# Output weights in dead columns of the spatial weights, loaded in the kv stage; four output buffers; two banks for the last spatial halves; a reordered start

## The chip, the cores and the metric

The kernel runs on one core of a Trainium2 chip. The metric is the time of one execution on the device, in microseconds, as the median of several executions. The span of a profiled execution (first to last instruction) is about 1.7 us shorter than its time.

## The reference

One input `x` (2048 tokens, 512 wide) goes through two mixers, and a gate blends them. Cut to what matters (the softmax, GELU and layer-norm helpers are the usual ones):

```python
g = sigmoid((x * gate_w).sum(-1, keepdims=True))

# A: linear attention, 32 heads of 16
q, k, v = split(x @ wqkv)                                  # per head
phi_q = concat(softmax(q @ w_phi), softmax(-(q @ w_phi)))  # and phi_k likewise
kv = phi_k.T @ v ;  z = phi_k.sum(over tokens)
a  = ((phi_q @ kv) / (phi_q @ z + 1e-6)) @ wo

# B: gated MLP with a spatial matmul over the 2048 tokens
z1, z2 = halves(gelu(x @ w_in))                            # 688 columns each
u = z1 * (w_sp @ layernorm(z2) + b_sp)
b = u @ w_out

out = g * a + (1 - g) * b
```

## The kernel before

It has three stages. The first computes `z1` and `z2` and folds `w_phi` into the q and k weights. The second, the kv stage, goes over 16 token tiles, accumulates `kv`, and runs one *spatial half* per tile (half of the 688 columns of `w_sp @ z2` for one output tile). The third runs the attention of each tile, the remaining spatial halves, the remaining q tiles, and the output matmuls, which add both mixers in one accumulator. Stores come in groups of four tiles.

The start. The first two tiles are transposed on TensorE; both halves of tile 1 go through one PSUM tile:

```python
tp1 = psA.tile([P, 2, 2 * CH], BF16, name="tp1", tag=next_turn("zp", 3))
# ... warm-up matmuls, transposes of tile 0 ...
one(0, 0, 0)              # one(tile, slab, half): one 128x344 matmul with w_in
for h in range(2):
    x_T(1, 2 * h, 2 * h + 2,
        tp1[:, h, 0:2 * P].rearrange("p (d n) -> p d n", n=P), on_act=h == 1)
one(0, 1, 0)
warm_up(2, P)
one(1, 0, 0)
one(1, 1, 0)
gate_T()                  # puts gate_w beside the weights, as a column of the second halves
for dt in range(2):
    one(0, dt, 1)
    one(1, dt, 1)
one(0, 2, 0)
one(1, 2, 0)
# ...
```

The output weights (1.9 MB) are loaded after the kv stage, into SBUF that the kv stage frees, on ScalarE's queue:

```python
def load_out_weights():
    slabs = outw.tile([P, 11 + NDT, D], BF16, name="slabs")
    # ... w_main, w_rem, wo_t are views of slabs ...
    nc.gpsimd.memset(w_rem, 0.0)
    nc.scalar.dma_start(out=wo_t, in_=A_wo.rearrange("(g p) n -> p g n", p=P))
    # ... four more nc.scalar.dma_start for w_out ...
```

One output tile is nine or ten matmuls of 512 columns. The rows that are left over of `w_out` are added per group, and then ScalarE evicts the four tiles of the group one after the other, each into one of two `ob` buffers, from which a DMA stores it:

```python
def ba_store(acc, tt, c0, c1, on_dve):
    ob = work.tile([P, c1 - c0], BF16, name=f"ob{c1 - c0}")      # pool of 2
    # ... last tile's tail on VectorE ...
        nc.scalar.activation(out=ob[:, :], in_=acc, func=AF.Copy, scale=g_inv[:, tt:tt + 1])
        nc.scalar.dma_start(out=dst, in_=ob[:, :])
```

The third stage, in which one bank serves all q tiles and one all spatial halves:

```python
gg_next(mm_tile())                      # one spatial half, evicted by VectorE
w_main, w_rem, wo_t = load_out_weights()
nq = len(Q_AT)                          # 6 q tiles were done in the kv stage
q_bank, g_bank, *acc_banks = [next_turn("mm", 6) for _ in range(6)]
attn_tile(0)                            # o -> DMA transpose -> oT
for i in range(NT - 1):
    if i + nq < NT:
        q_tile(i + nq, bank_tile(q_bank))   # ScalarE reads the bank twice (exp of +x and -x)
    gg_next(bank_tile(g_bank))
    attn_tile(i + 1)
    if i > 0:
        ba_step(i - 1)                  # output matmuls: needs oT and uT
ba_tile(14)
ba_tile(15, cuts=(0, 384, D))
```

The softmax here doesn't subtract the row's maximum and nothing guards it: scores larger than these inputs give would overflow.

## Time and profile before

| | before |
|---|---|
| time, median | 212.78 us (3 runs, 212.43 to 212.85) |
| span of the profile | 211.2 us |
| TensorE busy | 202.3 us, 96% |
| VectorE, ScalarE, GpSimd busy | 131.4, 75.4, 46.5 us |
| mean granted clock | 1.0 |

The page of the profile of the kernel before: busy microseconds by engine (PE is TensorE), and the span in 40 slices of 5.28 us, in which a digit is the busy share in tenths.

```profile
PE 202.3 (96%) x1438; PEld 121.6 (58%) x1456; DVE 131.4 (62%) x282; ACT 75.4 (36%) x122; POOL 46.5 (22%) x78
...
PE   7999999999999999999999996999989999899994
...
DMA  6999999999912024142221499753544368254342
```

TensorE has something to do almost all the time. The list of what its matmuls waited for is short. The columns are: engine and line that waited, what released it, microseconds in total, number of waits, longest wait. Line 460 is a spatial half, 369 a q or k tile, 497 and 499 the output matmuls.

```profile
PE mm L497 <- DMA oT<-o: 1.7, 1, 1.7
PE mm L369 <- ACT eq L373: 1.0, 1, 1.0
...
PE mm L460 <- DVE ucat L465: 0.6, 1, 0.6
PE tp L286 <- DVE xT L292: 0.4, 1, 0.4
PE zp L196 <- DVE w_z L297: 0.3, 1, 0.3
```

A matmul's wait says who came last, not why it was late. For that one follows the chain of waits (start us, duration us, what), here cut to the three places in the third stage where TensorE was not the one that everything waited for:

```profile
125.79 5.78 DMA oT<-o
131.61 1.04 PE mm L497 x4
...
150.28 0.69 ACT ob L513
150.98 2.43 DMA out_dram<-ob
153.50 0.70 ACT ob L513
...
155.81 1.09 ACT eq L373 x2
156.95 0.38 PE mm L369
...
174.36 4.09 DMA out_dram<-ob
...
180.88 1.09 ACT eq L373 x2
181.99 1.23 DVE zs L377
...
183.83 0.56 DVE ucat L465
184.44 2.49 PE mm L460 x16
```

The first place is the DMA transpose of `o` at 125.79, which took 5.78 us. In the second, an eviction (line 513) waits for a store that takes 2.43 us to release an `ob` buffer (ScalarE stands idle for 1.40 us of it); after this eviction and one more ScalarE comes to the exponentials of a q tile, and only then is the q bank free for line 369. In the third, the store takes 4.09 us and ScalarE waits 3.05, and there VectorE's reduction of the q tile (line 377) comes late too, stands before the eviction of a spatial half (line 465) in VectorE's program, and so line 460 gets its only bank late.

What the gaps cost is read from TensorE's own timeline as the distance between two starts, less what the same distance is elsewhere without a gap: 1.91 us at 131.61, 1.16 us at 156.95, 0.75 us at 184.44. This is a little more than the list of waits says, because a matmul's end in the profile reaches into the next one.

### The profile page before, as it was taken

Reading aid. Unit: us, or ns where it says so; the run is one execution under the profiler, and the core shown is the slowest. Engines: PE = TensorE matmul, PEld = TensorE weight load, DVE = VectorE, ACT = ScalarE, POOL = GpSimd, SP = SyncE. Lnnn points to the kernel's source line nnn. Section 1 sums busy time; section 2 is a strip of 40 time slices with the busy share of each in tenths; the row PEclk is TensorE's granted clock in tenths of the full one; section 3 lists DMA queues with packets and bytes.
Section 4 is the critical chain, followed back from the end, with each engine's and each line's share of the span. In section 5 each row is a group of like instructions: output and inputs, shape, how many; then the busy total and the mean of one; then the engine's idle time right before and its main releaser. Section 6 shows DMA issues by size and latency. Waiting matters only on the chain.

```text
span 211.2 us, 3762 instructions
## 1 busy us (share of the span) xinstructions
PE 202.3 (96%) x1438; PEld 121.6 (58%) x1456; DVE 131.4 (62%) x282; ACT 75.4 (36%) x122; POOL 46.5 (22%) x78
## 2 busy tenths in 40 slices
PE   7999999999999999999999996999989999899994
PEld 3666667765665555656555664555445555565642
DVE  3477685856977586979797669455356563443330
ACT  3666666676222333232323222222251122301322
POOL 7020202020623324424252422122204220100000
PEclk9999999999999999999999999999999999999999
DMA  6999999999912024142221499753544368254342
GB/s 189 267 137 198 250 290 215 274 274 211 260 37 42 0 39 79 21 77 51 41 50 37 75 288 220 137 112 74 121 116 90 75 113 128 75 112 90 101 112 75
DMA packets 88970, 27.20 MB, mean 129 GB/s; under 512 B 82968, under 2 KB 88952, under 8 KB 88952
## 3 DMA queue, kind: packets, MB, share of 16 engines
q1 hardware_dynamic: 84208, 22.43, 54.8%
q10 hardware_dynamic: 4712, 4.53, 7.3%
q8 instruction: 11, 0.18, 0.4%
q14 instruction: 7, 0.06, 0.1%
q0 software_dynamic: 32, 0.00, 0.0%
HBM read 4.41 MB, written 2.10 MB: 31 GB/s over the span
## 4 chain that ended last, share of the span: by engine, by line
PE 86%; DMA 6%; ACT 3%; DVE 1%; issue 1%; ACTq 1%; DVEq 0%
PE mm L460 31%; PE zp L196 18%; PE mm L369 12%; PE mm L499 7%; PE mm L409 7%; PE mm L497 5%; DMA out_dram<-ob 3%; DMA oT<-o 3%; ACT ob L513 2%; PE kvacc L425 2%; PE zp L227 2%; PE at L473 1%; ACT eq L373 1%; PE mm L502 1%; PE pq L321 1%
## 5 line engine op out<-in xcount | busy, mean ns | idle before, releaser
L460 PE MATMUL mm<-z2all,wspT 128*128 128x344 bf16 x512 | 79.9, 309 | 0.6 <-DVE ucat L465 0.6
L460 PEld LDWEIGHTS <-wspT 128*128 128x128 bf16 x512 | 49.0, 98 | 26.5 <-issue 1.3
L196 PE MATMUL zp<-w_z,xT 128*128 128x344 bf16 (+1 forms) x256 | 39.8, 309 | 0.3 <-DVE w_z L297 0.3
L373 ACT ACTIVATE eq<-mm 128x512 bf16<-128x512 f32 x32 | 17.4, 594 | 53.2 <-PE mm L369 25.2
L377 DVE TENSOR_REDUCE zs<-eq 128x64 f32<-128x1024 bf16 x16 | 19.5, 1219 | 24.0 <-ACT eq L373 24.0
L196 PEld LDWEIGHTS <-xT 128*128 128x128 bf16 x256 | 24.5, 98 | 11.5 <-issue 0.4
L465 DVE SCALAR_TENSOR_TENSOR ucat<-mm,bT,z1all 128x344 bf16<-128x344 f32 x32 | 17.5, 547 | 21.7 <-PE mm L460 21.7
L386 POOL TENSOR_TENSOR eq<-eq,ratio 128x512 bf16<-128x512 bf16 x16 | 16.9, 1058 | 52.8 <-DVE ratio L385 41.7
L373 ACT ACTIVATE ek<-mm 128x512 bf16<-128x512 f32 x32 | 17.3, 600 | 27.2 <-PE mm L369 27.2
L513 ACT ACTIVATE ob<-mm,g_inv 128x512 bf16<-128x512 f32 (+1 forms) x16 | 10.9, 680 | 34.6 <-PE mm L502 24.0
L377 DVE TENSOR_REDUCE zs<-ek 128x64 f32<-128x1024 bf16 x16 | 19.3, 1208 | 2.8 <-ACT ek L373 2.8
L369 PEld LDWEIGHTS <-xT 128*128 128x128 bf16 x128 | 12.2, 98 | 14.0 <-issue 1.3
L499 PE MATMUL mm<-slabs,uT 128*128 128x512 bf16 (+2 forms) x85 | 20.1, 366 | 0.0
L497 PE MATMUL mm<-slabs,oT 128*128 128x512 bf16 (+2 forms) x62 | 15.8, 365 | 2.1 <-DMA oT<-o 1.7
L369 PE MATMUL mm<-wq_p,xT 128*128 128x512 bf16 x55 | 16.0, 379 | 1.5 <-ACT eq L373 1.0
L386 POOL TENSOR_TENSOR ek<-ek,ratio 128x512 bf16<-128x512 bf16 x16 | 16.9, 1058 | 2.0 <-DVE ratio L385 1.2
L409 PE MATMUL mm<-wv_sb,xT 128*128 128x512 bf16 x64 | 16.4, 379 | 0.0
L369 PE MATMUL mm<-wk_p,xT 128*128 128x512 bf16 x61 | 16.1, 379 | 0.2
L214 DVE BATCH_NORM_STATS2 bn<-z2all 128x6 f32<-128x344 bf16 x32 | 14.9, 502 | 0.0
L211 ACT ACTIVATE z2all<-zp 128x688 bf16<-128x688 f32 x16 | 11.8, 744 | 7.0 <-PE zp L196 6.6
L266 ACT ACTIVATE z1all<-zp 128x688 bf16<-128x688 f32 x16 | 11.9, 744 | 6.7 <-PE zp L196 6.7
L499 PEld LDWEIGHTS <-uT 128*128 128x128 bf16 x85 | 8.1, 98 | 9.2
(80 smaller groups left out, 148.9 us busy)
## 6 DMA issues: line engine op xcount, KB each, us to landing
out_dram<-ob ACTq DMA_DIRECT2D x15, 128.0 KB, 1.9
slabs<-in_B_w_out_dram ACTq DMA_DIRECT2D x2, 640.0 KB, 8.2
w_z<-in_B_w_in_dram SPq DMA_DIRECT2D x2, 344.0 KB, 4.6
w_z<-in_B_w_in_dram ACTq DMA_DIRECT2D x3, 172.0 KB, 3.3
wv_sb<-in_A_wqkv_dram SPq DMA_DIRECT2D x1, 512.0 KB, 4.5
slabs<-in_A_wo_dram ACTq DMA_DIRECT2D x1, 512.0 KB, 3.8
xs<-in_A_x_dram SPq DMA_DIRECT2D x2, 128.0 KB, 3.3
xs<-in_A_x_dram SPq DMA_DIRECT2D x1, 256.0 KB, 5.0
```

The source lines that it names most:

```text
L196: nc.tensor.matmul(zp[:, j, 0:n], lhsT=xT[:, dt, tt * P:(tt + 1) * P], rhs=wt[:, dt, j * HF:j * HF + n], start=(dt == 0), stop=(dt == NDT ...
L214: nc.vector.bn_stats(out=bn6[:, tt, j, :], in_=z2v[:, j, :])
L369: nc.tensor.matmul(ps[:, :], lhsT=xT[:, dt, tt * P:(tt + 1) * P], rhs=w[:, dt, :], start=(dt == 0), stop=(dt == NDT - 1))
L373: nc.scalar.activation(out=e[:, :, a, :], in_=ps[:, :].rearrange("p (h f) -> p h f", f=DH), func=AF.Exp, scale=1.0 - 2.0 * a)
L377: nc.vector.tensor_reduce(out=z[:].rearrange("p h a -> p (h a)"), in_=e[:].rearrange("p h a f -> p (h a) f"), axis=AX.X, op=ALU.add,)
L386: nc.gpsimd.tensor_tensor(out=e[:, :, 1, :], in0=e[:, :, 1, :], in1=ratio[:, :, None].to_broadcast([P, H, DH]), op=ALU.mult)
L409: nc.tensor.matmul(v_ps[:, :], lhsT=xT[:, dt, tt * P:(tt + 1) * P], rhs=wv_sb[:, dt, :], start=(dt == 0), stop=(dt == NDT - 1))
L460: nc.tensor.matmul(gp[:, 0:HF], lhsT=wspT[:, st, tt * P:(tt + 1) * P], rhs=z2all[:, st, j * HF:(j + 1) * HF], start=(st == 0), stop=(st == ...
L465: nc.vector.scalar_tensor_tensor(out=ucat[tt % NU][:, c0 + j * HF:c0 + (j + 1) * HF], in0=gp[:, 0:HF], scalar=bT[:, tt:tt + 1], in1=z1all[ ...
L497: nc.tensor.matmul(acc, lhsT=oT[:, g, :], rhs=wo_t[:, g, c0:c1], start=(g == 0), stop=False)
L499: nc.tensor.matmul(acc, lhsT=uT[:, i + ft, :], rhs=w_main[i][:, ft, c0:c1], start=False, stop=False)
L513: nc.scalar.activation(out=ob[:, :], in_=acc, func=AF.Copy, scale=g_inv[:, tt:tt + 1])
```

## The change

Its intent: take the 1.9 MB of weights away from the beginning of the third stage, where they share the DMA engines with the transposes that the first output tile needs. After the eighth spatial half, the first 512 columns of the transposed spatial weights are dead; the output weights go there, in the middle of the kv stage. This frees SBUF for two more `ob` buffers. After the last q tile, its bank takes every second spatial half. The start is reordered: the two halves of tile 1 go through separate PSUM tiles, and two matmuls of the third slab fill the wait for the gate column. The diff, without the lines that only keep pools open longer:

```diff
@@ start
-        tp1 = psA.tile([P, 2, 2 * CH], BF16, name="tp1", tag=next_turn("zp", 3))
+        tp1 = psA.tile([P, 2, P], BF16, name="tp1", tag=next_turn("zp", 3))
@@
-        for h in range(2):
-            x_T(1, 2 * h, 2 * h + 2,
-                tp1[:, h, 0:2 * P].rearrange("p (d n) -> p d n", n=P), on_act=h == 1)
+        x_T(1, 0, 2, tp1[:, :, :])
+        x_T(1, 2, NDT, pq_tile([P, 2, P], BF16)[:, :, :], on_act=True)
         one(0, 1, 0)
@@
         gate_T()
+        one(0, 2, 0)
+        one(1, 2, 0)
         for dt in range(2):
             one(0, dt, 1)
             one(1, dt, 1)
-        one(0, 2, 0)
-        one(1, 2, 0)
@@ load_out_weights
-        slabs = outw.tile([P, 11 + NDT, D], BF16, name="slabs")
+        slabs = wspT[:, :, 0:D]
@@ (all five loads)
-        nc.scalar.dma_start(...)
+        nc.sync.dma_start(...)
@@ ba_store
-        ob = work.tile([P, c1 - c0], BF16, name=f"ob{c1 - c0}")
+        ob = work.tile([P, c1 - c0], BF16, name=f"ob{c1 - c0}", bufs=4 if c1 - c0 == D else 1)
@@ kv stage
             gg_next(mm_tile())
+            if tt == 7:
+                w_main, w_rem, wo_t = load_out_weights()
@@ third stage
-        w_main, w_rem, wo_t = load_out_weights()
@@
-            gg_next(bank_tile(g_bank))
+            gg_next(bank_tile(g_bank if i + nq < NT or i % 2 == 0 else q_bank))
```

More of the change, by code (lines that the diff above doesn't have):

```diff
@@ L55 @@
     pers = ctx.enter_context(tc.tile_pool(name="pers", bufs=1))
-    kvw_cm = tc.tile_pool(name="kvw", bufs=1, side="right")
-    kvw = kvw_cm.__enter__()
+    kvw = ctx.enter_context(tc.tile_pool(name="kvw", bufs=1, side="right"))
     early_cm = tc.tile_pool(name="early", bufs=1, side="right")
@@ L357 @@
     work = ctx.enter_context(tc.tile_pool(name="work", bufs=2, reuse_waits="tile"))
-    kvp_cm = tc.tile_pool(name="kvp", bufs=2, side="right", reuse_waits="tile")
-    kvp = kvp_cm.__enter__()
+    kvp = ctx.enter_context(tc.tile_pool(name="kvp", bufs=2, side="right", reuse_waits="tile"))
     def bank_tile(tag):
@@ L446, in load_out_weights @@
         nc.gpsimd.memset(w_rem, 0.0)
-        nc.scalar.dma_start(out=wo_t, in_=A_wo.rearrange("(g p) n -> p g n", p=P))
+        nc.sync.dma_start(out=wo_t, in_=A_wo.rearrange("(g p) n -> p g n", p=P))
         for i in range(2):
-            nc.scalar.dma_start(
+            nc.sync.dma_start(
                 out=w_main[i],
@@ L452, in load_out_weights @@
             )
-        nc.scalar.dma_start(out=w_rem[0:REM, :], in_=B_w_out[5 * P:FH, :])
-        nc.scalar.dma_start(out=w_rem[P - REM:P, :], in_=B_w_out[0:REM, :])
+        nc.sync.dma_start(out=w_rem[0:REM, :], in_=B_w_out[5 * P:FH, :])
+        nc.sync.dma_start(out=w_rem[P - REM:P, :], in_=B_w_out[0:REM, :])
         return w_main, w_rem, wo_t
@@ L570 @@
         kvz_evac()
-        kvp_cm.__exit__(None, None, None)
-        kvw_cm.__exit__(None, None, None)
-        outw = ctx.enter_context(
-            tc.tile_pool(name="outw", bufs=1, side="right", reuse_waits="tile"))
         gg_next(mm_tile())
-        w_main, w_rem, wo_t = load_out_weights()
         nq = len(Q_AT)
```

## The prediction

> **What bounds it now.** TensorE: the page of the kernel before gives matmuls 202.3 of 211.2 us (96%), granted clock 1.0. Only gaps in its stream can be won. In TensorE's timeline and the chain of waits they are:
>
> 1. Start: 0.4 us before the second pair of input transposes of tile 1 (VectorE still copies out of the same PSUM tile), 0.3 us for the gate column.
> 2. 129.7 to 131.6: the first output matmul (L497) waits for the transpose of o, which took 5.8 us from issue to landing; the median is 2.5. It shares the DMA engines with 1.9 MB of output weights, issued at 120.5 to 124.2 (8.2 us to land). Cost in the chain 1.9 us.
> 3. 155.8 to 156.95: the next q matmul (L369) waits for a bank that ScalarE must read. ScalarE first does four output evictions; the third waits 1.4 us for one of two ob buffers. Cost 1.16 us.
> 4. 183.7 to 184.44: a spatial half (L460) waits for its only bank. VectorE evicts it after a reduction (L377) that waits for ScalarE, which had waited 3.05 us for an ob buffer. Cost 0.75 us.
>
> The first 0.8 and last 3.1 us stay.
>
> **What the change does.**
> - Weights are issued after the eighth spatial half (ends 81.8), when DMA share is 2 to 4 tenths, and are needed 48 us later. The Trainium skill ("Trainium Kernel Development and Optimization", Key Constraints) says the SP, ACT and POOL queues run on the same 16 DMA engines; so the earlier moment counts, not the other queue. The trace agrees: loads on ACT's queue slowed a transpose on SP's. Transpose of o then lands at about 128.2, before its use: -1.9. The memset (0.53 us) now delays GpSimd at 82, where ek has slack: 0.
> - Four ob buffers: evictions follow every 1.15 us, so four and the exponentials (1.08) take 5.7 us from 150.27, to 155.95, 0.2 after TensorE is ready: -0.95.
> - With ScalarE 2.6 us earlier in the second group, and a second bank, gap 4 goes: -0.75.
> - Start: the 0.4 goes; the gate wait is filled by two matmuls of the third weight slab, but that lands only at 6.2 (issue 1.76, 4.4 to land), some 0.3 us of new waiting: net -0.35.
> - New cost: VectorE's order changes at 124 to 127 us. The reduction of q tile 6 now stands before the eviction of a spatial half, so its bank comes free at about 127.1, when TensorE wants it at 126.8: +0.15.
>
> No instruction's duration changes. Sum: -1.9 -0.95 -0.75 -0.35 +0.15 = -3.8 us, all on TensorE's chain, dense after each gap.
>
> **Prediction: 209.0 us (212.78 - 3.8), 208.2 to 210.2 with 8 in 10.** Faster by over 2% (below 208.5): 0.2; within 2%: 0.79; slower: 0.01.
>
> **What would show it.** TensorE idle falls from 8.9 us to about 5; busy stays 202. The list of waits has no output matmul waiting for the transpose of o, no ob waiting for a store, at most 0.3 us for q matmuls on ScalarE. Longest landing of that transpose: under 3.5 us. DMA share rises around 82 to 92 us instead of 120 to 132.
>
> **What would make it wrong.** Weights on SP's queue hold up transposes of eq and u; the start waits for weight slabs; the first q matmuls after the kv stage meet a larger bank wait; or the dense stream exposes a next limit (VectorE, 62% busy, or the o transposes).

## The result, and the profile after

| | before | after |
|---|---|---|
| time, median | 212.73 us (4 runs, 212.43 to 212.85) | 209.18 us (4 runs, 208.92 to 209.80) |
| ratio | 1 | 0.9839, 95% interval 0.9815 to 0.9863 |
| span of the profile | 211.2 us | 207.5 us |
| TensorE busy | 202.3 us | 203.6 us |

A ratio is the mean time of one kernel's fast runs over that of the other's of the same rounds, so it is not quite the ratio of the medians in the table. The change is a gain of 1.6%, under the 2% that would count as faster, and 0.2 us from the predicted 209.0.

The page after, the same lines as before:

```profile
PE 203.6 (98%) x1456; PEld 122.5 (59%) x1456; DVE 131.4 (63%) x282; ACT 75.4 (36%) x122; POOL 46.6 (22%) x78
...
PE   8999999999999999999999999999999999999994
...
DMA  6999999999922014971403236753564469253442
```

TensorE's row has no slice under 9 tenths any more between the first and the last. In the DMA row the weights now stand in slices 16 and 17, counted from 0 (83 to 93 us), and the two full slices of before, 23 and 24 (121 to 132 us), are down to 3 and 6 tenths. TensorE's list of waits, which leaves out the shortest, has one line left, the first matmul of the program:

```profile
PE zp L226 <- PEq L597: 0.8, 1, 0.8
```

The chain of waits answers to the three places. Lines 494, 366 and 457 are what 497, 369 and 460 were; now the chain stays on TensorE from the first matmul to the last.

```profile
129.86 0.86 PE mm L494 x4
...
154.02 0.97 PE mm L366 x4
...
180.89 2.33 PE mm L457 x16
```

The chain lets a piece begin where the one before it ends, so its starts are up to 0.2 us later than those of the timeline.

In TensorE's timeline the first output matmul starts at 129.69 (131.61 before), the q tile after the first stores at 153.97 (156.95) and the spatial half at 180.72 (184.44). The lead therefore grows from 0 to 1.92, 2.98 and 3.72 us, and the last matmul starts 3.70 us earlier (204.21 for 207.91). So the whole gain lies in those three steps: 1.92, 1.06 and 0.74 us. The start brought nothing in this pair of profiles. The transpose of `o` that the first output matmul needs landed in 2.5 us, where it had taken 5.8:

```profile
L483 SPq DMA_TRANSPOSE oT<-o x1: 1242/1242/1242, 125.5 to 125.5; - x1
...
DMA to landing us min/median/max: 2.5/2.5/2.5
```

The same queue holds a transpose of `eq` just ahead of it, issued at 124.19 before and at 124.17 after. That one took 6.8 us before and 3.2 after, and that of `o` landed about half a microsecond behind it both times. So both were late together.

### The profile page after: what moved, and what is told of

Read it like the earlier page. It is cut to its first block, busy times and chain, and to the rows that moved or that the text cites. A ratio compares the mean times of both kernels' runs of the same rounds, so it can differ in the third digit from the quotient of the medians.

```text
span 207.5 us, 3776 instructions
## 1 busy us (share of the span) xinstructions
PE 203.6 (98%) x1456; PEld 122.5 (59%) x1456; DVE 131.4 (63%) x282; ACT 75.4 (36%) x122; POOL 46.6 (22%) x78
## 4 chain that ended last, share of the span: by engine, by line
PE 98%; DVE 0%; issue 0%
PE mm L457 36%; PE zp L195 18%; PE mm L366 13%; PE mm L496 8%; PE mm L494 7%; PE mm L406 7%; PE at L470 2%; PE kvacc L422 2%; PE zp L226 2%; PE mm L499 1%; PE pq L319 1%; PE pq L284 1%; DVE ob L506 0%; PE pq L305 0%; PE tp L284 0%
## 5 line engine op out<-in xcount | busy, mean ns | idle before, releaser
L195 PE MATMUL zp<-w_z,xT 128*128 128x344 bf16 (+1 forms) x256 | 40.6, 312 | 0.0
L195 PEld LDWEIGHTS <-xT 128*128 128x128 bf16 x256 | 24.7, 99 | 11.2
L496 PE MATMUL mm<-wspT,uT 128*128 128x512 bf16 (+2 forms) x85 | 20.1, 366 | 0.0
L494 PE MATMUL mm<-wspT,oT 128*128 128x512 bf16 (+2 forms) x68 | 16.6, 366 | 0.0
```

Source lines behind the costliest of these rows:

```text
L195: nc.tensor.matmul(zp[:, j, 0:n], lhsT=xT[:, dt, tt * P:(tt + 1) * P], rhs=wt[:, dt, j * HF:j * HF + n], start=(dt == 0), stop=(dt == NDT ...
L494: nc.tensor.matmul(acc, lhsT=oT[:, g, :], rhs=wo_t[:, g, c0:c1], start=(g == 0), stop=False)
L496: nc.tensor.matmul(acc, lhsT=uT[:, i + ft, :], rhs=w_main[i][:, ft, c0:c1], start=False, stop=False)
```

## The experiments

Ten of the twelve runs take the change apart or put one cost back, one repeats the kernel before, and the last is a version that the others suggest. Each was timed in five rounds beside the kernel before. They ran in four groups on four chips, with medians of the kernel before of 212.25, 212.35, 212.14 and 212.37 us, so a run is compared by its ratio, and in fine detail by its trace. All were correct. Two executions were slow and are left out of the ratios: one of before_ob4 (213.69 us, clock 0.991) and one of before_wearly (434.75 us).

The table has, for every kernel with a fast profile, the cost of each gap, read from TensorE's starts as above, and the start of the third tile's first matmul, which ends the part that the start reorders. In the column of the q gap, 0.11 to 0.16 us is left in all eight profiles with four buffers. There ScalarE's exponentials end just after TensorE is ready, and the q matmul starts 0.05 us after their end.

| kernel | ratio (95%) | gap before the first output matmul | q gap | spatial-half gap | third tile starts |
|---|---|---|---|---|---|
| before, first profile | 1 | 1.91 | 1.16 | 0.75 | 8.78 |
| before_again | 1.0008 (0.9985 to 1.0031) | 0.89 | 1.21 | 0.52 | 8.89 |
| before_newstart | 0.9971 (0.9949 to 0.9992) | 0.89 | 1.19 | 0.68 | 8.54 |
| before_ob4 | 0.9914 (0.9890 to 0.9938) | 1.34 | 0.16 | 0 | 8.99 |
| late_traffic | 0.9887 (0.9862 to 0.9913) | 1.27 | 0.16 | 0 | 8.35 |
| w_late_act | 0.9880 (0.9851 to 0.9908) | 0.59 | 0.16 | 0 | 8.57 |
| w_early_act | 0.9859 (0.9830 to 0.9887) | 0 | 0.16 | 0 | 8.30 |
| ob2 | 0.9878 (0.9852 to 0.9904) | 0 | 1.25 | 0 | 8.27 |
| ob2_onebank | 0.9945 (0.9916 to 0.9974) | 0 | 1.36 | 0.69 | 9.20 |
| onebank | 0.9848 (0.9825 to 0.9872) | 0 | 0.11 | 0 | 9.07 |
| oldstart | 0.9869 (0.9849 to 0.9889) | 0 | 0.11 | 0 | 9.07 |
| after | 0.9839 (0.9815 to 0.9863) | 0 | 0.11 | 0 | 8.84 |
| gate_early | 0.9832 (0.9805 to 0.9859) | 0 | 0.12 | 0 | 8.39 |

### Is it the traffic of the weights that delays the transpose?

The theory is that the loads and the transpose share the DMA engines. The rivals are that the first output tile waited for the weights themselves, or that the order of VectorE's program, which differs between the two kernels at that place, made the difference. **late_traffic** keeps the change, so the weights are in place early, and adds the same loads once more at the old moment, into columns 512 to 1023 of the spatial weights, which are dead by then. Nobody reads them.

```diff
         gg_next(mm_tile())
+        spare = wspT[:, :, D:2 * D]
+        nc.scalar.dma_start(out=spare[:, 11:15, :], in_=A_wo.rearrange("(g p) n -> p g n", p=P))
+        # ... and the four loads of w_out likewise ...
         nq = len(Q_AT)
```

> The changed kernel, with the same 1.9 MB loaded a second time at the old moment, on ScalarE's queue, into columns of the spatial weights that are dead by then and that nobody reads. Contention theory: the first output matmul waits again for the transpose of o (1 to 2.5 us, landing over 4.5 us), so about 211.1 us, ratio to before about 0.992. Rival (the late arrival of the weights themselves, or VectorE's changed order, made the old gap): no wait, 209.2 us, ratio 0.984. Waits on ob buffers stay gone in both.

Measured: 210.02 us, ratio 0.9887. In its profile, a line of TensorE's waits, and then one of the chain:

```profile
PE mm L494 <- DMA oT<-o: 1.1, 1, 1.1
```

```profile
125.05 5.38 DMA oT<-o
```

The gap is back, 1.27 us by the starts, although no instruction depends on the added loads. The transpose took 5.4 us (5.8 in the first profile of before), and the expectation of 1.9 us for the gap was too high. The first rival falls: the real weights were in place. The second does not fall by this run alone, because VectorE's order changed along with the loads: here, as in every kernel that loads late, it evicts the spatial half first (125.70) and then reduces the q tile (127.24), and in every kernel that loads early it is the other way round (reduction at 125.02, eviction at 126.55 in the changed kernel). What speaks against it is the time of issue. In late_traffic the transposes of `eq` and `o` were issued at 123.67 and 125.05, no later than in the changed kernel (124.17 and 125.50), since TensorE runs 0.5 us ahead there. Only the time from issue to landing grew, for `eq` from 3.2 to 6.3 us, and in the program no instruction of VectorE stands between the issue of a transpose and its landing. So it is the traffic that delays the transposes, by this argument and not by the run alone; no profile has the early load with the old order.

**w_late_act** puts the one real load back to the old moment and ScalarE's queue:

```diff
@@ load_out_weights (all five loads)
-        nc.sync.dma_start(...)
+        nc.scalar.dma_start(...)
@@ kv stage
-            if tt == 7:
-                w_main, w_rem, wo_t = load_out_weights()
@@ third stage
         gg_next(mm_tile())
+        w_main, w_rem, wo_t = load_out_weights()
```

> The changed kernel, with the one real load of the output weights put back to the old moment and ScalarE's queue (still into the dead columns). Contention theory: about 1.9 us back, all before the first output matmul: 211.1 us, ratio 0.992; the waits on ob buffers stay gone. Rival (the gain came from somewhere else, such as VectorE's order or the freed SBUF): 209.2 us, ratio 0.984.

Measured: 209.64 us, ratio 0.9880, with a gap of 0.59 us. The direction is right, the size of 1.9 us is not. The same load at the same moment cost 1.91, 0.89, 0.89, 1.34 and 0.59 us in five profiles: how badly a transpose of 2.5 us is hit (4.7 to 5.8 us in the five) differs from execution to execution.

**w_early_act** keeps the early moment and changes the queue only (the first hunk of the diff above alone).

> The changed kernel, loading early but on ScalarE's queue. Theory (the moment counts, not the queue): no wait at the first output matmul; ScalarE spends some 3.7 us issuing at 82 us and its exponentials come later, which costs TensorE 0 to 0.5 us: 209.2 to 209.7 us, ratio 0.983 to 0.986. Rival (SP's queue is part of the gain): at least 1 us slower than the changed kernel, ratio 0.988 or more.

Measured: 209.27 us, ratio 0.9859, no gap before the first output matmul. It ran in the same group as w_late_act and is 0.2% faster, about 0.4 us, in line with the 0.59 us gap, though the intervals overlap, and its own reaches the rival's 0.988; it is the trace that decides. ScalarE issues the five loads in the kv stage without harm to TensorE. So the moment counts and the queue does not, which fits what the Trainium skill says ("Trainium Kernel Development and Optimization", Key Constraints: the queues run on the same 16 DMA engines).

**before_wearly** is the kernel before with the early load alone, made from the changed kernel by taking back all else:

```diff
-        ob = work.tile([P, c1 - c0], BF16, name=f"ob{c1 - c0}", bufs=4 if c1 - c0 == D else 1)
+        ob = work.tile([P, c1 - c0], BF16, name=f"ob{c1 - c0}")
@@
-            gg_next(bank_tile(g_bank if i + nq < NT or i % 2 == 0 else q_bank))
+            gg_next(bank_tile(g_bank))
@@ and the start as in the kernel before
```

> The kernel before with the early load alone (two ob buffers, one bank for the last halves, the old start). Theory: only the gap before the first output matmul goes, 1.9 us: 210.8 us, ratio 0.991; the q matmul still waits about 1.1 us and the spatial half about 0.7 us. Rival (gaps grow later when an earlier one goes, so that the parts only work together): less than 1 us, ratio above 0.995.

Measured: ratio 0.9949 (0.9918 to 0.9980) from five fast runs, about 1.1 us. By the time alone it lies between theory and rival. Its profile can't be used for the gaps: it fell into an execution of 434.75 us, which is treated at the end. But ob2_onebank below differs from it only by the new start, and its profile decides: no gap before the first output matmul, and later gaps of 1.36 and 0.69 us, against 1.16 to 1.21 and 0.52 to 0.75 in the three profiles with two buffers, one bank and the late load. So the later gaps grow by at most some 0.2 us, and it is the theory with a smaller size.

### Which of buffers and bank closes the two later gaps?

**ob2** gives back the two `ob` buffers, **onebank** the one bank, **ob2_onebank** both:

```diff
-        ob = work.tile([P, c1 - c0], BF16, name=f"ob{c1 - c0}", bufs=4 if c1 - c0 == D else 1)
+        ob = work.tile([P, c1 - c0], BF16, name=f"ob{c1 - c0}")
```

```diff
-            gg_next(bank_tile(g_bank if i + nq < NT or i % 2 == 0 else q_bank))
+            gg_next(bank_tile(g_bank))
```

> The changed kernel with two ob buffers again. Theory: the q matmul after the first group of stores waits about 1.1 us again; ScalarE is late by over 2 us in the second group too, but the second bank lets TensorE pass, so nothing there: 210.2 us, ratio 0.988. Rival (the buffers alone count, the bank does nothing): both waits come back, 1.8 us, 211.0 us, ratio 0.992.

> The changed kernel with one bank for the last spatial halves. Theory: with four ob buffers ScalarE is early enough, the bank is free 2 us before it is wanted, and the second bank is worth nothing: 209.2 us, ratio 0.984, no wait of a spatial half on VectorE. Rival (the bank is part of the gain): a wait of about 0.7 us, 209.9 us, ratio 0.987.

> The changed kernel with two ob buffers and one bank. Theory: the waits of 1.1 us (q matmul) and 0.7 us (spatial half) both come back: 211.0 us, ratio 0.992. If the bank was never worth anything it equals the run with two ob buffers alone.

Measured: ob2 209.65 us (0.9878), onebank 209.13 us (0.9848), ob2_onebank 211.06 us (0.9945). TensorE's waits of ob2, and then of ob2_onebank:

```profile
PE mm L366 <- ACT eq L370: 1.1, 1, 1.1
```

```profile
PE zp L195 <- DMA w_z<-in_B_w_in_dram: 1.3, 1, 1.3
PE mm L366 <- ACT eq L370: 1.2, 1, 1.2
...
PE mm L457 <- DVE ucat L462: 0.5, 1, 0.5
```

With two buffers the q gap is back. ScalarE waits for a store in the second group too (its first wait there is 2.99 us in ob2), but with a second bank TensorE goes past. Only where the bank is taken away as well does the spatial half wait. With four buffers the second bank is not needed for anything: onebank has no wait of a spatial half, and its q gap is that of the changed kernel. From onebank to ob2_onebank, in the same group, the ratio rises by 0.0097, or 2.06 us of 212.35; the two gaps there are 1.36 and 0.69, together 2.05 us. So four buffers are worth both gaps, and the second bank is an insurance for the second of them, worth nothing beside four buffers.

**before_ob4** is the kernel before with four buffers alone:

```diff
-        ob = work.tile([P, c1 - c0], BF16, name=f"ob{c1 - c0}")
+        ob = work.tile([P, c1 - c0], BF16, name=f"ob{c1 - c0}", bufs=4 if c1 - c0 == D else 1)
```

> The kernel before with four ob buffers alone. Theory: both later waits go (1.1 and 0.7 us), the wait for the transpose of o stays at 1.9 us: 210.9 us, ratio 0.9915. Rival (four buffers need the second bank or the early load): 1.1 us or less, ratio 0.995 or more.

Measured: 210.57 us, ratio 0.9914, which is 1.8 us. In the third stage its profile has one wait of TensorE left:

```profile
PE mm L497 <- DMA oT<-o: 1.2, 1, 1.2
```

The buffers need neither the bank nor the early load, and with 1.8 us they are the largest part of the change. It also shows that a little SBUF was free all along: the buffers did not have to wait for the weights to move.

### What is the start worth?

**before_newstart** is the kernel before with the new start, **oldstart** the changed kernel with the old one, by the same edit backward. **before_again** is the kernel before, unchanged, for a second profile.

```diff
-        tp1 = psA.tile([P, 2, 2 * CH], BF16, name="tp1", tag=next_turn("zp", 3))
+        tp1 = psA.tile([P, 2, P], BF16, name="tp1", tag=next_turn("zp", 3))
@@
-        for h in range(2):
-            x_T(1, 2 * h, 2 * h + 2, ...)          # both halves through tp1
+        x_T(1, 0, 2, tp1[:, :, :])
+        x_T(1, 2, NDT, pq_tile([P, 2, P], BF16)[:, :, :], on_act=True)
@@ the two matmuls one(0, 2, 0) and one(1, 2, 0) go to just after gate_T()
```

> The changed kernel with the old order of the first two tiles. The prediction's step: 0.35 us slower, 209.5 us, and the third tile's first matmul 0.35 us later in the trace at the same clock. Rival A (the start is set by where TensorE's slow first microseconds end, which differs from run to run): times equal on average, and in the traces the start follows the moment of the switch, not the order. Rival B: the new order is worth nothing even at equal clock.

> The kernel before with the new order of the first two tiles alone. The prediction's step: 0.35 us faster, 212.4 us, ratio 0.998. Rival A and B: ratio 1.000 within 0.001. In the trace: no wait of the second transposes on VectorE; where TensorE is fast from 4 us on, the third tile's first matmul should come at about 8.4 us, against 8.78 in the profile of before.

> The kernel before, unchanged, for a second profile. Rival A expects that the moment at which the first matmuls become fast differs from 4.0 us by up to 3 us, and that the third tile's first matmul moves with it; if both stay where they were (4.0 and 8.78 us), rival A has no support here. Ratio 1.000 within 0.002.

Measured: oldstart 209.37 us, ratio 0.9869; before_newstart 211.50 us, ratio 0.9971; before_again 212.03 us, ratio 1.0008.

The traces tell more than the times. Here is TensorE's timeline of the first microseconds in before, in the changed kernel and in ob2, which has the same start as the changed kernel (start us, duration us, line, what, number of matmuls). "pq<-ident,xs" are transposes of 128 columns, "zp" matmuls of 344. The last line of each is the third tile.

```profile
4.00 0.40 PE L286 MATMUL pq<-ident,xs 128*128 128x128 bf16 x4
...
4.55 0.32 PE L196 MATMUL zp<-w_z,xT 128*128 128x344 bf16 x1
...
5.46 0.27 PE L286 MATMUL tp<-ident,xs 128*128 128x128 bf16 x2 [0.38 <-DVE xT L292]
...
6.58 1.33 PE L196 MATMUL zp<-w_z,xT 128*128 128x345 bf16 x8 [0.29 <-DVE w_z L297]
...
8.78 0.89 PE L196 MATMUL zp<-w_z,xT 128*128 128x344 bf16 x5
```

```profile
3.89 0.63 PE L284 MATMUL pq<-ident,xs 128*128 128x128 bf16 x4
...
4.64 0.49 PE L195 MATMUL zp<-w_z,xT 128*128 128x344 bf16 x1
...
5.85 0.78 PE L195 MATMUL zp<-w_z,xT 128*128 128x344 bf16 x2
...
6.50 1.48 PE L195 MATMUL zp<-w_z,xT 128*128 128x344 bf16 x8
...
8.84 0.89 PE L195 MATMUL zp<-w_z,xT 128*128 128x344 bf16 x5
```

```profile
3.90 0.63 PE L284 MATMUL pq<-ident,xs 128*128 128x128 bf16 x4
...
4.93 0.28 PE L284 MATMUL tp<-ident,xs 128*128 128x128 bf16 x2
...
5.92 1.48 PE L195 MATMUL zp<-w_z,xT 128*128 128x344 bf16 x8
...
8.27 1.48 PE L195 MATMUL zp<-w_z,xT 128*128 128x344 bf16 x9
```

Four transposes take 0.40 us in before and 0.63 in the changed kernel; one matmul of 344 columns 0.32 and 0.49. TensorE is slow at first and becomes fast at some moment, and this moment is different in each execution: by single matmuls, about 3.7 us in before, 4.3 in before_again, 5.1 in before_ob4, about 6.5 in the profile of the changed kernel, about 4.9 in ob2. The Trainium skill ("TensorE: Matmul & The Clock Gate", What's actually happening) describes this: the array's clock is halved until the engine has been busy through a window of about 3.4 us, and the window runs freely, so that the switch falls at another place in every run. The trace agrees in two points: over thirteen profiles the switch falls between 3.6 and 6.5 us, and matmuls of 128 columns start 0.107 us apart before it and 0.056 after (the durations in the profile, which overlap, differ 1.6 times). It does not bear out a whole busy window: the earliest switch came 2.8 us after the first matmul. The profile's mean granted clock reads 1.000 all the same.

So rival A of the expectation holds for single profiles: the changed kernel was unlucky by a late switch, and its start gained nothing against a lucky before. But the order has a worth: the two waits of the old start, 0.38 and 0.29 us in the timeline of before, are in all four profiles with it and in none of the eight with the new one. The old start has its third tile at 8.78, 8.89, 8.99 and 9.07 us (mean 8.93), the new one in eight profiles at 8.27 to 9.20 (mean 8.64). The mean difference is 0.29 us, close to the predicted 0.35; with so few profiles its own 95% interval is about 0 to 0.6. before_newstart was timed at 0.3% (0.6 us) faster, an interval of 0.1 to 0.5%, and oldstart's ratio is 0.3% above the changed kernel's, from another group and with overlapping intervals; this is too little to say that it is more than 0.29.

Two of the eight are as late as the old start: onebank (9.07) and ob2_onebank (9.20), which had an early switch. Both wait for the third weight slab, 0.9 and 1.3 us (the line "PE zp L195 <- DMA w_z" of ob2_onebank above). There the prediction's worry came true in a larger size: the matmuls that fill the wait for the gate need a slab that sometimes lands only at 7.0 us, and eight matmuls then stand behind it. In w_late_act it landed at 6.33 and cost about 0.3 us, as predicted; in the other five, at 5.3 to 5.9, it cost nothing.

**gate_early** is made from this. The gate's matmul goes ahead of tile 1's, so that its column is ready without any filler, and the third slab comes after the four matmuls that it held up:

```diff
         one(0, 1, 0)
+        gate_T()
         warm_up(2, P)
         one(1, 0, 0)
         one(1, 1, 0)
-        gate_T()
-        one(0, 2, 0)
-        one(1, 2, 0)
         for dt in range(2):
             one(0, dt, 1)
             one(1, dt, 1)
+        one(0, 2, 0)
+        one(1, 2, 0)
```

> The changed kernel with the gate matmul moved ahead of tile 1's first matmuls, and the four second-half matmuls of slabs 0 and 1 put back ahead of the third slab. Two earlier profiles of the new start waited 0.9 and 1.3 us for the third slab with eight matmuls still to do behind it; here only four are behind it, so in such an execution the third tile should start about 0.6 us earlier (by 8.6 instead of 9.1 to 9.2 us), and in the others no later than the new start (8.3 to 8.6 us). No wait of TensorE for the gate column. Time: 0 to 0.4 us below the changed kernel, ratio to before 0.982 to 0.985, which the noise may hide; the trace decides. Rival (the start is limited by the slow first microseconds alone): third tile no earlier than with the new start at the same moment of the switch, and no gain.

Measured: 208.65 us, ratio 0.9832 (0.9805 to 0.9859). No wait for the gate, none for the slab, third tile at 8.39 us although its input tiles landed late (it waited twice 0.2 us for them). It has the lowest median of all, and it beats the kernel before; that it beats the changed kernel is not shown, since the intervals cover each other and no slow slab fell into its profile (the third landed at 6.29).

## Why the prediction was right

The time was predicted as 209.0 us and measured as 209.18, the class as within 2%, which it is. Term by term, in the pair of profiles and over all runs:

| step | predicted | in this pair of profiles | over all runs |
|---|---|---|---|
| transpose of `o` no longer beside the weights | -1.9 | -1.92 | -0.6 to -1.9; the early load alone timed at -1.1 |
| four buffers, q gap | -0.95 | -1.06 | -1.0 to -1.1 (gap 1.16 to 1.21 in before, 0.11 to 0.16 with four buffers) |
| buffers and bank, spatial-half gap | -0.75 | -0.74 | -0.5 to -0.75, all of it from the buffers |
| start | -0.35 | 0 | -0.29 in the mean of the profiles |
| VectorE's new order | +0.15 | 0 | 0: no gap in any of the seven profiles with it |
| sum | -3.8 | -3.70 | measured -3.4 by the ratio |

- *What bounds it* was right. TensorE's gaps are the whole story: the groups of instructions on the page kept their mean durations within 1%, and the 3.70 us are the three gaps.
- *The traffic* was right in mechanism: late_traffic brings the delay back, and the times of issue speak against a part of VectorE's order in it. Its size was read from one profile, which was the worst of five. This is the mis-sized term: 1.9 predicted, about 1.1 in before_wearly (0.4 to 1.7 by its interval). That the total still came out within 0.2 us is in part luck: this size is at the upper end of what other executions show, and in the pair the 0.35 us that the start did not bring were mostly made up by 0.15 us that VectorE's order did not cost and 0.11 us more from the q gap.
- *The buffers* were right and slightly under-sized. The prediction allowed 0.2 us of remaining wait for the q tile, and 0.11 to 0.16 us of it is there in all eight profiles with four buffers. Here the Trainium skill's hint applies ("Perfetto Trace Analysis", Optimization Strategy: consistent bubbles can mean that the next tile has no buffer): the two bubbles, one for each group of stores that has q tiles behind it, went with two more buffers, but for these 0.11 to 0.16 us.
- *The bank* was put together with the buffers for gap 4. It is worth nothing beside them.
- *The start* was right on average and wrong for the profile at hand. The moment of the clock's switch moves it by more than the reorder does: ob2, with the same start and the switch 1.6 us earlier, has its third tile 0.57 us earlier than the changed kernel. The third slab cost nothing in five of the eight profiles, about 0.3 us in one, and 0.9 and 1.3 us in two, where the prediction had 0.3 us always.
- *VectorE's order* cost nothing. In the changed kernel's timeline the eviction in question ends at 127.03 us and the matmul that wants the bank starts at 127.10. The margin is only 0.07 us, so the worry was near to the truth.
- *The signs* came as told: TensorE's idle time fell from 8.9 to 3.9 us (5 was expected), no eviction waits for a store, the traffic moved to 82 to 92 us. TensorE's busy time rose by 1.3 us instead of staying; the trace has 1456 matmuls after and 1438 before, so a part of this may be records that are missing before, and a part the slower start; the parts were not separated.

The last term that remains open is the difference between -3.70 in the profiles and -3.4 by the ratio. The interval of the ratio (-2.9 to -3.9 us) holds both.

## What to carry to other kernels

When one engine is busy 96% of the time, list its few gaps, find out for each what came last and why that was late, and add them up: here the sum was the gain to be had. What paid here: move bulk loads to a stage where nobody waits for a small DMA, and look for SBUF that is dead by then; give a group of stores as many output buffers as the group has tiles before adding banks. Size a gap that comes from shared DMA engines, and anything in the first microseconds, from several profiles, as one profile can show twice or none of it.

## What the Trainium skill lacked or had wrong

- "DMA: Bandwidth & Descriptors" (Rules for kernel authors) says of order and safety that a transpose next to ordinary DMAs needs nothing, and no page gives the price in time. Here a transpose of 128 by 512 elements, with a median of 2.5 us to landing, took 4.7 to 5.8 us beside 1.9 MB of loads on the other queue (w_late_act, and the first profile of before), a different amount in each execution, and landed close behind another transpose that was slowed too. (Without such loads one of the sixteen took 4.4 to 4.6 us as well, in each of the seven profiles with the early load, where TensorE did not wait for it; no run here shows why.)
- "TensorE: Matmul & The Clock Gate" gives the switch as some 4 us into sustained work, give or take half a microsecond (What you observe), and as set by a free-running window (What's actually happening). In thirteen profiles with the same warm-up it came between 2.8 and 5.7 us after the first matmul (3.6 to 6.5 us of the span). The half microsecond is too narrow for this kernel. The spread of 2.9 us fits a window that runs freely.
- The same page's caveat that the clock gate was seen stuck for over 50 us may be what one execution here shows, for longer. In before_wearly's profile TensorE stayed slow to the end: 434.75 us instead of 211, spatial matmuls of 526 ns mean instead of 309, while the profile gave a mean granted clock of 1.0. It was one of more than a hundred executions, the kernel's other five took 210.7 to 211.8 us, and no run here shows its cause. Its page:

```profile
span 433.0 us, 3761 instructions
...
L458 PE MATMUL mm<-z2all,wspT 128*128 128x344 bf16 x512 | 167.1, 526 | 0.0
```

- It belongs on that page too that the profile's mean granted clock does not show the slow first stretch: it reads 1.000 in the changed kernel's profile, where TensorE was slow until 6.5 us. The duration of a matmul of known shape does show it: 0.32 us against 0.49 for the first of 128x344.
